# A new hand-written order for the first run of an attention and mixture-of-experts kernel, with other engines for some of its operations

## The chip, the core and the metric

The kernel runs on one core of a Trainium2 chip. The metric is the device time of one execution in microseconds (us). The kernel before takes 992.88 us, the median of three runs (991.37, 992.88 and 993.13). The profile is of one more execution, which took 993.18 us.

## The reference

The computation is causal attention over 4 batches, 8 heads, 576 positions and 64 dimensions per head, mixed per head with a linear memory branch, and then four experts over all 2304 rows of the result:

```python
a = softmax(causal(scale * q @ k.T));  local = a @ v        # per batch and head
phi = lambda x: where(x > 0, x, exp(x) - 1) + 1
mem = (phi(q) @ M_prev) / (phi(q) . z_prev + 1e-6)
g = 1 / (1 + exp(-beta))
x = (g * mem + (1 - g) * local)          # to (B*S, H*D) = (2304, 512)
p = probs / (probs.sum(-1) + 1e-9)
out = sum over 4 experts e of p[:, e] * (relu(x @ w1[e]) @ w2[e])   # 512 -> 1024 -> 512
```

Everything is float32. The expert products are computed as three products of a high part and a low part of each operand (`xh`, `xl`, `w`, `hh`, `hl`).

## The kernel before, in words

The order of all work is written by the kernel itself; no scheduler reorders it. The attention is cut into runs of one batch and two or three blocks of 128 positions. The expert work is cut into phases: a phase takes half an expert's hidden units, computes `h` (`mm1`, matmuls at L889, evicted by ScalarE as `hh` at L898 and by VectorE as `hl` at L899) and then `y` (`mm2`, L920). The weights come by DMA into `stg`, and `w_prep` (L212) splits each 128x512 piece into a high part (L227 on Pool, or L225 on ScalarE) and a low part (L228 on Pool). While TensorE works at the phases, the attention of later runs is put between their matmuls by a planner with costs and due times; its tasks are pairs of heads of a run (`t_trq`, `t_trk`, `t_phi1` to `t_phi4`, `j_qk` and so on).

The phases need a first run of attention to start on: batch 0, positions 0 to 255, all 8 heads. This is `first_run` (L1253). Its order is the list of words `ORDER`, and each word with its number is a call of a local function: `tr` transposes q and k of a pair of heads, `cq` and `ck` bring them from PSUM to SBUF, `sc` multiplies them (pair 0..3 and query block 0..1 make the numbers 0..7), `mk` masks and takes the row maximum on VectorE, `ex` is the exponential with its sum on ScalarE, `rc` the reciprocals on VectorE, `nm` the scaling of the exponentials by 1/sum on ScalarE (L1350; 16 of them, one for each of the 8 blocks and 2 heads), `pt` and `pe` transpose the probabilities and evict them, `r`, `e`, `p`, `z`, `rr`, `rn`, `m` are the memory branch (z and m on Pool, p, rr, rn on VectorE), `tq` and `eq` transpose its q and evict it, `ou` multiplies with the values and the memory, `xh` and `xl` split the result, `w` is one `w_prep` (both parts on Pool), `go` runs the planner's steps that are due before the first phase, and `d` is a pair of dummy matmuls of zeros, 128x512, on TensorE.

The first task of the next run (index 0) starts within the first run by `go`: `t_phi2` puts `qp` on VectorE (L314) and `zb`, `rl` on Pool (L319, L323, L326), and `t_phi3` puts the reduction `rn` on VectorE (L339). `t_trq` and `t_trk` of this task transpose its q and k (`tq`, `tk`), split them on ScalarE and VectorE (L366, L369, L372, L379, L385), and `t_cpk` copies halves of `khb` and `kha` by DMA on ScalarE's queue. Its first scores are `sp` (L486).

In PSUM, `h` and `y` share the tag `moe`, which has three banks: the fourth `h` of a phase takes the bank of the first, once `hh` and `hl` of the first have been read from it. The `after()` call in `mm1` issues a planner's step that follows the `h`. `c_probs2` (L868 to L873) normalises the experts' probabilities on VectorE (`psm`, `pn`). The start of the kernel has the zeros for the dummies, the identity and the masks; six dummy matmuls `ids` stand ahead of the list.

Of the kernel before, what the change touches and what calls it, by code (L numbers as in the profile page):

```python
# [10 lines left out]
AF = mybir.ActivationFunctionType  # L11
ALU = mybir.AluOpType
# [37 lines left out]
def tile_attention_moe(  # L50
# [344 lines left out]
    def flat(ap):  # L395
        return ap.rearrange("p j d -> p (j d)")

    def t_trq(t):
        pt = to_tile(f"tq{t.i}")
        qk, last = t.qk, t.nk == NCH  # L400
        w = len(t.cs) * P
        for i in range(len(t.cs)):

            tr(pt[:, i * P : (i + 1) * P], flat(t.nat["q"][:, i]), P)
        if last:
            tr(pt[:, w : w + P], flat(t.nat["k"][:, 4]), P)
# [341 lines left out]
    def ev(slot, prio, fn, cost=0.0, vec=0.0):  # L748
        wt = PR["wvec"] + PR["wpe"] * cost + vec
        events.setdefault(slot, []).append((prio, len(events.get(slot, [])), fn, wt))  # L750

    def dv(n):
        return 150.0 + n / 0.96

    seen = set()
    for t in tasks:
        s0 = t.s0
        ld = -9 + t.i if t.i < 2 else s0 - 7
        PQ = PR
        n = len(t.cs)  # L760
        if t.run not in seen:
            seen.add(t.run)
            ev(s0 - 9, 9 if t.i else 6, lambda r=t.run: batch_load(r))
            ev(s0 - (5 if t.i else 8), 9, lambda r=t.run: batch_load_m(r))
            ev(s0 + (2 if t.joint else 3), 9 if t.joint else 0.1, lambda r=t.run: batch_prep(r))
            if t.cs == CB and t.b == 0:
                for i in range(2):
                    ev(s0 - 12, 9, lambda i=i: zeros(i))
        if t.joint:
            ev(ld, 6.3, lambda t=t: t_load(t))  # L770
        else:
# [12 lines left out]
        ev(s0 + PQ["trq"][0], PQ["trq"][1], lambda t=t: t_trq(t), 109.0 * n, 2 * dv(n * P))
        ev(s0 + PQ["trk"][0], PQ["trk"][1], lambda t=t: t_trk(t), 109.0 * t.nk, 2 * dv(4 * P))
        if not t.joint:
            ev(s0 + PQ["trq"][0] + 1, 0.5, lambda t=t: t_cpq(t))
            ev(s0 + PQ["trk"][0], 2.4, lambda t=t: t_cpk(t))
        ev(s0, PQ["v"], lambda t=t: t_v(t))
        ev(  # L790
            s0 + PQ["trqp"][0 if t.joint else 2],
            PQ["trqp"][1],
            lambda t=t: t_trqp(t),
            109.0 * n,
            2 * dv(t.nq),
        )
# [446 lines left out]
    def first_run():  # L1243
# [9 lines left out]
        qT, kT, tf, pf, st, ptp, pw, tpf, of = ({} for _ in range(9))  # L1253
        qpw = [xr[:, a, 4 * P : 6 * P] for a in range(NPAIR)]

        def load(dst, src, c, h0, h1):
            nc.sync.dma_start(
                out=dst[:, c, h0:h1],
                in_=src[b, h0:h1, c * P : (c + 1) * P].rearrange("h p d -> p h d"),
            )  # L1260
# [87 lines left out]
        def f_nm(i, hd):  # L1348
# [2 lines left out]
                s_[:, hd], s_[:, hd], AF.Copy, scale=t_[:, 4 + hd : 5 + hd]  # L1351
            )

        def f_pt(i):
            s_ = st[i][0]
            c = i % 2
            ptp[i] = (
                moe_bank(f"ptf{i}")
                if c
                else ps.tile([P, 512], F32, tag="pt", name=f"ptf{i}", bufs=1)  # L1360
            )
            pt4 = ptp[i][:, 0 : 2 * (c + 1) * P].rearrange("p (h j q) -> p h j q", h=2, q=P)
            for hd in range(2):
                for j in range(c + 1):
                    tr(pt4[:, hd, j], s_[:, hd, j * P : (j + 1) * P], P)

        def f_pe(i):
            n = 2 * (i % 2 + 1) * P
            t_ = sp.tile([P, DM], F32, tag="acc", name=f"ptw{i}", bufs=4)
            if i % 2:  # L1370
                nc.vector.tensor_copy(t_[:, 0:n], ptp[i][:, 0:n])
            else:
                nc.scalar.activation(t_[:, 0:n], ptp[i][:, 0:n], AF.Copy)
# [70 lines left out]

        def f_w(j):
            w_prep(0, "1" if j < HF else "2", True)
            if j in (1, 3):
                while si[0] < len(steps) and steps[si[0]][0] <= (-9 if j == 1 else -8):
                    run_step()

        def f_go(j):
            while si[0] < len(steps) and steps[si[0]][0] <= -j:
                run_step()

        def f_d(j):
            z_ = moe_bank(f"id{j}")
# [1 line left out]
                nc.tensor.matmul(z_, lhsT=hh[0][:, 0:P], rhs=hh[0], start=True, stop=True)  # L1458

        ORDER = """  # L1460
        tr0 cq0 ck0 sc0 mk00 ex00 mk01 sc1 tr1 mk10 ex01 d11 mk11 rc0 ex10 cq1 ex11
        ck1 d4 nm00 sc3 rc1 nm01 r1 sc2 pt0 e1 nm10 tr3 mk20 mk30 mk21 mk31 tr2 nm11
        pt1 ck3 cq2 p1 ck2 pe1 sc4 mk40 r0 mk41 d0 d1 e0 z1 d6 ex31 ex21 p0 d13 d8
        ex20 d3 ex30 rr1 z0 rc2 ex40 d7 d10 cq3 d5 nm21 pe0 ex41 rc3 rn1 rr0 ldv w0
        rc4 sc5 nm20 pt2 rn0 sc7 m1 mk50 nm30 nm31 m0 sc6 mk51 pe2 pt3 nm40 nm41
        ex50 ex51 tq0 w1 mk70 pe3 mk71 w2 rc5 eq0 tq1 eq1 w3 ex70 pt4 mk60 ou0 w4 d9
        ex71 nm51 tq3 mk61 xh0 nm50 rc7 xl0 eq3 d2 ex61 nm71 pt5 ex60 rc6 nm70 pe4
        nm60 nm61 pe5 tq2 ou1 pt7 w5 eq2 pt6 pe7 xh1 ou2 xl1 pe6 w6 ou3 go5 xh2 xl2
        xh3 xl3 go4 w7 d12
        """  # L1470
        calls = {k[2:]: g for k, g in locals().items() if k.startswith("f_")}

        nc.scalar.dma_start(out=betab, in_=beta.partition_broadcast(P))
        nc.scalar.activation(psm[:, 0:1], ident[:, 0:1], AF.Exp)
        for h0, h1 in ((0, 2), (2, 4), (4, 8)):
            for c in range(2):
                load(qF, q, c, h0, h1)
                load(kF, k, c, h0, h1)
        nc.sync.dma_start(out=zb, in_=z_prev[b : b + 1].partition_broadcast(P)[:, 0])
        for _ in range(NSTG):  # L1480
            w_dma()
# [152 lines left out]
```

## Time and profile before

| | us |
|---|---|
| median of 3 runs | 992.88 (991.37 to 993.13) |
| the profiled execution | 993.18 |
| its span in the profile | 991.4 |
| TensorE (PE) busy | 982.5 |
| VectorE (DVE) busy | 648.2 |
| Pool busy | 591.3 |
| ScalarE (ACT) busy | 567.0 |
| first expert matmul `h` starts (from the start of the span) | 32.78 |
| first expert matmul `y` starts | 40.40 |

The profiled execution is 1.78 us longer than its span. Times in the rows are counted from the start of the span. A row of the timeline reads: start, duration (of all instructions in the row, from the first start to the last end), engine, line, operation, output and input tiles, form, count, and in brackets the idle time of that engine just before with what ended it. The ends of matmuls are modelled: the distance between two starts is the better measure of what one costs.

### The profile page before, as it was taken

Reading aid. Unit: us, or ns where it says so; the run is one execution under the profiler, and the core shown is the slowest. Engines: PE = TensorE matmul, PEld = TensorE weight load, DVE = VectorE, ACT = ScalarE, POOL = GpSimd, SP = SyncE. Lnnn points to the kernel's source line nnn. Section 1 sums busy time; section 2 is a strip of 40 time slices with the busy share of each in tenths; the row PEclk is TensorE's granted clock in tenths of the full one; section 3 lists DMA queues with packets and bytes.
Section 4 is the critical chain, followed back from the end, with each engine's and each line's share of the span. In section 5 each row is a group of like instructions: output and inputs, shape, how many; then the busy total and the mean of one; then the engine's idle time right before and its main releaser. Section 6 shows DMA issues by size and latency. Waiting matters only on the chain.

```text
span 991.4 us, 16041 instructions
## 1 busy us (share of the span) xinstructions
PE 982.5 (99%) x5118; PEld 825.3 (83%) x5118; DVE 648.2 (65%) x1668; ACT 567.0 (57%) x1350; POOL 591.3 (60%) x601
## 2 busy tenths in 40 slices
PE   8999999999999999999999999999999999999998
PEld 6899878878888888888888888888888888888887
DVE  6788888887877788877777787745244153442533
ACT  7787866766666677866666665544324243242430
POOL 5898856666754667955665465486363562645620
PEclk9999999999999999999999999999999999999999
DMA  6766554454443356554543332141111111111102
GB/s 154 180 191 176 136 147 128 130 142 120 129 115 98 93 140 185 165 134 108 124 124 102 91 100 77 44 137 55 53 54 43 54 54 54 54 42 54 54 1 85
DMA packets 185268, 102.16 MB, mean 103 GB/s; under 512 B 96224, under 2 KB 163552, under 8 KB 185184
## 3 DMA queue, kind: packets, MB, share of 16 engines
q1 hardware_dynamic: 184880, 101.00, 37.5%
q8 instruction: 41, 0.67, 0.3%
q14 instruction: 43, 0.35, 0.1%
q10 hardware_dynamic: 304, 0.14, 0.1%
HBM read 90.09 MB, written 4.72 MB: 96 GB/s over the span
## 4 chain that ended last, share of the span: by engine, by line
PE 92%; DVE 3%; issue 1%; ACT 1%; DMA 1%; POOL 1%; POOLq 0%; ACTq 0%; DVEq 0%
PE h L889 21%; PE y L920 20%; PE y L1197 18%; PE x L1119 9%; PE z L1119 4%; PE pt L353 4%; PE sp L624 4%; PE o L734 3%; PE y L1119 2%; PE o L572 1%; PE sp L486 1%; PE tk L353 1%; PE tq L353 1%; PE tp L353 1%; PE id L1458 1%
## 5 line engine op out<-in xcount | busy, mean ns | idle before, releaser
L228 POOL TENSOR_TENSOR w2l<-stg,w2h 128x512 fp32r<-128x512 f32 x128 | 167.6, 1314 | 153.3 <-ACT w2h L225 148.6
L889 PE MATMUL h<-xh,w 128*128 128x512 f32 (+1 forms) x768 | 245.8, 370 | 0.0
L228 POOL TENSOR_TENSOR w<-stg,w 128x512 fp32r<-128x512 f32 x96 | 126.8, 1325 | 147.8 <-ACT w L225 130.2
L889 PEld LDWEIGHTS h<-xh,w 128*128 128x128 f32 x768 | 138.7, 189 | 17.6 <-POOL w L228 0.3
L889 PE MATMUL h<-xl,w 128*128 128x512 f32 (+1 forms) x384 | 136.4, 355 | 0.0
L920 PE MATMUL y<-w2h,hh 128*128 128x512 f32 x320 | 135.7, 424 | 0.1
L920 PE MATMUL y<-w2h,hl 128*128 128x512 f32 x320 | 126.3, 395 | 0.0
L920 PE MATMUL y<-w2l,hh 128*128 128x512 f32 x320 | 125.9, 393 | 0.2
L1214 DVE SCALAR_TENSOR_TENSOR acc<-y,pn,acc 128x512 f32<-128x512 f32 (+1 forms) x57 | 41.6, 740 | 82.3 <-PE y L1197 82.3
L673 ACT ACTIVATE pth<-pt 128x384 fp32r<-128x384 f32 (+3 forms) x128 | 50.3, 420 | 62.7 <-PE pt L353 61.6
L889 PEld LDWEIGHTS h<-xl,w 128*128 128x128 f32 x384 | 72.9, 190 | 5.8
L920 PEld LDWEIGHTS y<-w2h,hl 128*128 128x128 f32 x320 | 60.0, 188 | 14.3 <-DVE hl L899 0.8
L898 ACT ACTIVATE hh<-h 128x512 fp32r<-128x512 f32 (+1 forms) x96 | 50.4, 525 | 36.4 <-PE h L889 34.5
L920 PEld LDWEIGHTS y<-w2l,hh 128*128 128x128 f32 x320 | 60.6, 189 | 9.5 <-POOL w2l L228 2.4
L920 PEld LDWEIGHTS y<-w2h,hh 128*128 128x128 f32 x320 | 60.4, 189 | 8.1 <-issue 0.5
L899 DVE SCALAR_TENSOR_TENSOR hl<-h,hh 128x512 fp32r<-128x512 f32 (+1 forms) x96 | 57.5, 599 | 13.3 <-ACT hh L898 11.9
L353 PE MATMUL pt<-ident,s 128*128 128x128 f32 (+1 forms) x376 | 60.8, 272 | 0.2
L353 PEld LDWEIGHTS pt<-ident,s 128*128 128x128 f32 (+1 forms) x376 | 46.9, 139 | 14.2 <-ACT s L669 0.5
L1143 DVE TENSOR_TENSOR cp_a<-y,cp_a 128x512 f32<-128x512 f32 x16 | 11.1, 692 | 71.4 <-PE y L1119 71.4
L225 ACT ACTIVATE w<-stg 128x512 fp32r<-128x512 f32 x92 | 57.0, 625 | 0.7
L675 DVE TENSOR_TENSOR ptl<-pt,pth 128x384 fp32r<-128x384 f32 (+1 forms) x96 | 51.5, 550 | 8.1 <-ACT pth L673 5.6
L648 ACT ACTIVATE s<-s,st 128x384 f32<-128x384 f32 (+2 forms) x80 | 54.7, 684 | 2.2 <-DVE st L632 1.9
(274 smaller groups left out, 2570.5 us busy)
## 6 DMA issues: line engine op xcount, KB each, us to landing
stg<-in_moe_w_dram SPq DMA_DIRECT2D x256, 256.0 KB, 2.9
natall<-in_k_dram SPq DMA_DIRECT2D x34, 128.0 KB, 2.6
natall<-in_v_dram SPq DMA_DIRECT2D x32, 128.0 KB, 3.1
natall<-in_q_dram SPq DMA_DIRECT2D x60, 64.0 KB, 2.8
out_dram<-acc SPq DMA_DIRECT2D x15, 256.0 KB, 2.0
kha<-kha SPq DMA_DIRECT2D x16, 128.0 KB, 2.3
khb<-khb SPq DMA_DIRECT2D x16, 128.0 KB, 2.3
natall<-in_k_dram SPq DMA_DIRECT2D x28, 64.0 KB, 2.6
```

What stands on the lines that cost most here:

```text
L225: nc.scalar.activation(hi, t, AF.Copy)
L228: nc.gpsimd.tensor_tensor(lo, t, f(hi), ALU.subtract)
L353: nc.tensor.transpose(dst, src, ident[0:n, 0:n])
L648: nc.scalar.activation(s.s[:, 0:w], s.s[:, 0:w], AF.Exp, bias=s.st[:, 0:1], scale=-1.0, accum_out=s.st[:, 2:3],)
L673: nc.scalar.activation(dh, src, AF.Copy)
L675: nc.vector.tensor_tensor(dl, src, f(dh), ALU.subtract)
L889: nc.tensor.matmul(pt[0][:, cols], lhsT=w_[:, c], rhs=x_[:, c, cols], start=(c == 0 and z == 0), stop=(c == NKD - 1 and z == 2),)
L898: nc.scalar.activation(h_, pt[0][:, cols], AF.Relu)
L899: nc.vector.scalar_tensor_tensor(l_, pt[0][:, cols], 0.0, f(h_), ALU.max, ALU.subtract)
L920: nc.tensor.matmul(pt[0], lhsT=h_[fc][:, tk], rhs=w_, start=(fc == 0 and z == 0), stop=(fc == HF - 1 and z == 2),)
L1119: nc.tensor.matmul(k_, lhsT=w_[:, c], rhs=x_[:, c], start=new and n == 0, stop=n == 5, skip_group_check=True,)
L1197: nc.tensor.matmul(y0, lhsT=a[:, tk], rhs=w_[:, x0:x1], start=(fc == 0 and z == 0), stop=(fc == HF - 1 and z == 2),)
```

## The change

The change replaces `ORDER` and adds functions for its new words. Of the 16 scalings, nine are done by Pool (`np`), two by VectorE (`nd`), five stay with ScalarE (`nm`). The scaled q of pairs 0 and 1 is evicted by VectorE (`cv`) instead of ScalarE, all four k by ScalarE (`ka`) instead of VectorE; the evictions of probabilities are five on ScalarE and three on VectorE instead of four and four, those of the memory branch's q two and two instead of four on ScalarE. The first task's `tk`, `kh`, `kl`, `tx`, `qh`, `ql` are words of the list now, and the planner's events for them are dropped. The first two loads of k are issued on ScalarE's queue, ahead of its table load, and the load of beta on Pool's queue. There are two pairs of dummies ahead of the list instead of three, and 14 within it as before. The word `w1` no longer issues planner steps; `go9` does. Cut to its core:

```diff
@@ planner @@
-        ev(s0 + PQ["trq"][0], PQ["trq"][1], lambda t=t: t_trq(t), 109.0 * n, 2 * dv(n * P))
-        ev(s0 + PQ["trk"][0], PQ["trk"][1], lambda t=t: t_trk(t), 109.0 * t.nk, 2 * dv(4 * P))
+        if t.i:
+            ev(s0 + PQ["trq"][0], PQ["trq"][1], lambda t=t: t_trq(t), 109.0 * n, 2 * dv(n * P))
+            ev(
...
@@ first_run @@
+        def f_cv(a):
+            nc.vector.tensor_scalar(qT[a], tf[a][0][:, 0:GW], SCALE, None, ALU.mult)
+        def f_ka(a):
+            by_act(kT[a], tf[a][1][:, 0:GW])
+        def f_np(i, hd):
+            s_, t_ = st[i]
+            nc.gpsimd.tensor_scalar(
+                s_[:, hd], s_[:, hd], t_[:, 4 + hd : 5 + hd], 1.0, ALU.mult, ALU.mult
+            )
+        def f_nd(i, hd):
+            s_, t_ = st[i]
+            nc.vector.tensor_scalar(
+                s_[:, hd],
+                s_[:, hd],
+                t_[:, 4 + hd : 5 + hd],
+                None,
+                ALU.mult,
+                ALU.max,
+                accum_out=dump,
+            )
         def f_w(j):
             w_prep(0, "1" if j < HF else "2", True)
-            if j in (1, 3):
-                while si[0] < len(steps) and steps[si[0]][0] <= (-9 if j == 1 else -8):
-                    run_step()
+            if j == 3:
+                f_go(8)
+        def f_tk(i):
+            tp_["k"] = to_tile("tk0")
+            for c in range(2):
+                tr(tp_["k"][:, c * P : (c + 1) * P], flat(tasks[i].nat["k"][:, c]), P)
+        def f_kh(i):
+            k_hi(tp_["k"], tasks[i].qk, 0, GW)
+            t_cpk(tasks[i])
+        def f_kl(i):
+            k_lo(tp_["k"], tasks[i].qk, 0, GW, True)
...
         ORDER = """
-        nm60 nm61 pe5 tq2 ou1 pt7 w5 eq2 pt6 pe7 xh1 ou2 xl1 pe6 w6 ou3 go5 xh2 xl2
-        xh3 xl3 go4 w7 d12
...
+        rc2 np30 ex40 tq0 nm31 eq1 nd20 w0 pt3 mk50 eq0 tq3 np21 mk51 ex41 ex50 rc4
+        ex51 ev3 pa3 rc5 ou0 pt2 mk60 xh0 pv2 np41 np40 nm50 tq2 mk61 sc7 xl0 pt4
+        mk70 ex60 mk71 ev2 ex61 np51 w1 pt5 pv4 ou1 w2 w3 pa5 ex71 rc6 ex70 w4 w5 ou2
+        rc7 xh1 nm61 xl1 w6 nm71 nm60 nd70 pt7 pt6 xh2 pa7 xl2 tk0 kh0 pv6 ou3 kl0
+        xh3 tx0 qh0 xl3 d12 w7 d3 d11 ql0 go5 go4
         """
-        nc.scalar.dma_start(out=betab, in_=beta.partition_broadcast(P))
+        for c in range(2):
+            load(kF, k, c, 0, 2, nc.scalar)
         nc.scalar.activation(psm[:, 0:1], ident[:, 0:1], AF.Exp)
         for h0, h1 in ((0, 2), (2, 4), (4, 8)):
             for c in range(2):
                 load(qF, q, c, h0, h1)
-                load(kF, k, c, h0, h1)
+                if h0:
+                    load(kF, k, c, h0, h1)
...
-        for j in range(3):
+        for j in range(2):
             f_d(f"s{j}")
...
     make_identity(nc, ident)
+    nc.gpsimd.dma_start(out=betab, in_=beta.partition_broadcast(P))
```

What this does to Pool's row of instructions is seen at two places. The first is Pool's memory branch and first weights. L1390 is `z` and L1405 is `m` (L1430 and L1445 after the change); `w` and `stg` are a `w_prep`; `sf` is a block of exponentials, scaled by L1369 after the change. Before:

```order
L1390 TENSOR_TENSOR xr<-xr,zbf 128x4x128 x2
L227 TENSOR_SCALAR w_109<-stg_159 128x512
L228 TENSOR_TENSOR w_109<-stg_159,w_109 128x512
L1405 TENSOR_TENSOR xr<-xr,rnf_143 128x4x128
L1405 TENSOR_TENSOR xr<-xr,rnf_142 128x4x128
```

After:

```order
L1369 TENSOR_SCALAR sf_203<-sf_203,stf_204 128x128 x2
L1369 TENSOR_SCALAR sf_225<-sf_225,stf_226 128x256 x2
L1430 TENSOR_TENSOR xr<-xr,zbf 128x4x128 x2
L1445 TENSOR_TENSOR xr<-xr,rnf_144 128x4x128
L1445 TENSOR_TENSOR xr<-xr,rnf_143 128x4x128
L1369 TENSOR_SCALAR sf_258<-sf_258,stf_259 128x256
L227 TENSOR_SCALAR w_109<-stg_159 128x512
L228 TENSOR_TENSOR w_109<-stg_159,w_109 128x512
L1369 TENSOR_SCALAR sf_274<-sf_274,stf_275 128x128
L1369 TENSOR_SCALAR sf_343<-sf_343,stf_344 128x128 x2
L1369 TENSOR_SCALAR sf_388<-sf_388,stf_389 128x256
```

Four scalings stand ahead of `z` now, and five behind `m`, around the first `w_prep`.

The second place is Pool's last two weights of the first run and the first task's memory branch (`zb`, `rl`). Before:

```order
L227 TENSOR_SCALAR w2h_114<-stg_421 128x512
L228 TENSOR_TENSOR w2l_115<-stg_421,w2h_114 128x512
L319 TENSOR_TENSOR zb_0_405<-zb_0_405,gate 128x512
L323 TENSOR_TENSOR rl_554<-qp_553,zb_0_405 128x4x64
L326 TENSOR_SCALAR rl_554<-gate 128x4
L227 TENSOR_SCALAR w2h_116<-stg_433 128x512
L228 TENSOR_TENSOR w2l_117<-stg_433,w2h_116 128x512
L345 TENSOR_TENSOR qp_553<-qp_553,rn_596 128x256
```

After:

```order
L227 TENSOR_SCALAR w2h_114<-stg_470 128x512
L228 TENSOR_TENSOR w2l_115<-stg_470,w2h_114 128x512
L227 TENSOR_SCALAR w2h_116<-stg_474 128x512
L228 TENSOR_TENSOR w2l_117<-stg_474,w2h_116 128x512
L319 TENSOR_TENSOR zb_0_331<-zb_0_331,gate 128x512
L323 TENSOR_TENSOR rl_578<-qp_577,zb_0_331 128x4x64
L326 TENSOR_SCALAR rl_578<-gate 128x4
L345 TENSOR_TENSOR qp_577<-qp_577,rn_583 128x256
```

The eighth `w_prep` stood behind `rl`, and stands ahead of it now.

The third place is VectorE around the first `hl`, which frees the PSUM bank for the fourth `h`. L899 is L906 after the change, L870 to L873 are L877 to L880. `rn` reads the `rl` of Pool. Before:

```order
L339 TENSOR_REDUCE rn_596<-rl_554 128x4
L340 RECIPROCAL rn_596<-rn_596 128x4
L899 SCALAR_TENSOR_TENSOR hl_105<-h_0_586,hh_101 128x256
L870 TENSOR_REDUCE psm<-pn 128x8
L871 TENSOR_SCALAR psm<-psm 128x8
L872 RECIPROCAL psm<-psm 128x8
L873 TENSOR_TENSOR pn<-pn,psm 128x32
L314 SCALAR_TENSOR_TENSOR qp_616<-natall,ex_613 128x256
```

After:

```order
L339 TENSOR_REDUCE rn_583<-rl_578 128x4
L340 RECIPROCAL rn_583<-rn_583 128x4
L877 TENSOR_REDUCE psm<-pn 128x8
L878 TENSOR_SCALAR psm<-psm 128x8
L879 RECIPROCAL psm<-psm 128x8
L880 TENSOR_TENSOR pn<-pn,psm 128x32
L314 SCALAR_TENSOR_TENSOR qp_604<-natall,ex_598 128x256
L906 SCALAR_TENSOR_TENSOR hl_105<-h_0_586,hh_101 128x256
```

`hl` stood directly behind `rn`, and now has the four instructions of the experts' probabilities and the next `qp` ahead of it.

## Rows read from the trace of the kernel before

**Rows 1.** The page, parts 1 and 4: busy time of the engines; chain that ended last.

```profile
PE 982.5 (99%) x5118; PEld 825.3 (83%) x5118; DVE 648.2 (65%) x1668; ACT 567.0 (57%) x1350; POOL 591.3 (60%) x601
...
PE 92%; DVE 3%; issue 1%; ACT 1%; DMA 1%; POOL 1%; POOLq 0%; ACTq 0%; DVEq 0%
```

**Rows 2.** Busy time by stretch: length, then each engine, granted clock, DMA share, GB/s.

```profile
0.00:5.24 5.24, 3.78 (x10) 2.72 (x10) 1.78 (x6) 2.18 (x5) 3.66 (x15) 1.00 0.38 83
...
32.78:40.40 7.62, 6.78 (x57) 6.62 (x57) 6.46 (x21) 4.19 (x14) 6.62 (x11) 1.00 0.85 206
40.40:100.00 59.60, 59.27 (x410) 53.67 (x409) 49.46 (x173) 48.26 (x130) 51.59 (x54) 1.00 0.65 177
100.00:991.40 891.40, 886.55 (x4484) 743.64 (x4482) 571.63 (x1392) 490.77 (x1132) 511.73 (x506) 1.00 0.35 95
```

**Rows 3.** Timeline of TensorE from 29.5 to 48 us.

```profile
32.78 0.36 PE L889 MATMUL h<-xh,w 128*128 128x256 f32 x1
...
37.95 0.30 PE L486 MATMUL sp<-khb,qb 128*128 128x128 f32 x1 [0.84 <-DMA khb<-khb]
...
38.19 0.33 PE L889 MATMUL h<-xh,w 128*128 128x256 f32 x1
...
40.40 0.40 PE L920 MATMUL y<-w2h,hh 128*128 128x512 f32 x1
```

**Rows 4.** Timeline of Pool from 0 to 40 us.

```profile
13.69 1.27 POOL L1390 TENSOR_TENSOR xr<-xr,zbf 128x512 f32<-128x512 f32 x1 [9.28 <-DVE xr L1386]
15.77 1.29 POOL L1390 TENSOR_TENSOR xr<-xr,zbf 128x512 f32<-128x512 f32 x1 [0.81 <-DVE xr L1386]
...
34.02 0.73 POOL L323 TENSOR_TENSOR rl<-qp,zb 128x256 f32<-128x256 f32 x1
34.81 0.20 POOL L326 TENSOR_SCALAR rl<-gate 128x4 f32<-128x4 f32 x1
35.10 0.62 POOL L227 TENSOR_SCALAR w2h<-stg 128x512 fp32r<-128x512 f32 x1
...
37.06 0.62 POOL L345 TENSOR_TENSOR qp<-qp,rn 128x256 f32<-128x256 f32 x1
...
39.23 0.40 POOL L448 TENSOR_SCALAR v<-natall 128x256 fp32r<-128x256 f32 x1
```

**Rows 5.** Timeline of VectorE from 27 to 42 us.

```profile
29.56 1.53 DVE L314 SCALAR_TENSOR_TENSOR qp<-natall,ex 128x256 f32<-128x256 f32 x1 [0.36 <-ACT ex L308]
...
35.39 0.42 DVE L339 TENSOR_REDUCE rn<-rl 128x4 f32<-128x260 f32 x1
...
36.05 0.42 DVE L899 SCALAR_TENSOR_TENSOR hl<-h,hh 128x256 fp32r<-128x256 f32 x1
36.40 0.17 DVE L870 TENSOR_REDUCE psm<-pn 128x8 f32<-128x32 f32 x1
...
37.64 0.41 DVE L314 SCALAR_TENSOR_TENSOR qp<-natall,ex 128x256 f32<-128x256 f32 x1
```

**Rows 6.** Timeline of TensorE from 0 to 16 us.

```profile
1.45 2.93 PE L1458 MATMUL ids<-hh 128*128 128x512 f32 x6 [1.45 <-DVE hh L1500]
4.17 0.63 PE L353 MATMUL tf<-ident,natall 128*128 128x128 f32 x2
...
5.84 1.65 PE L1294 MATMUL pf<-tw,tw 64*128 64x128 f32 x8 [0.61 <-DVE tw L1283]
...
14.50 1.86 PE L1458 MATMUL id<-hh 128*128 128x512 f32 x7
```

**Rows 7.** Timeline of SyncE's queue to 14 us, the load of z_prev.

```profile
6.96 0.50 SPq L1479 DMA_DIRECT2D zbf<-in_z_prev_dram  x1
```

**Rows 8.** DMA issues to 20 us: KB each, median us from issue to landing.

```profile
zbf<-in_z_prev_dram SPq DMA_DIRECT2D x1, 256.0 KB, 4.8
```

**Rows 9.** Timeline of ScalarE to 9 us, the first reader of beta.

```profile
3.77 0.21 ACT L1487 ACTIVATE ebp<-betab 128x8 f32<-128x8 f32 x1 [1.06 <-DMA betab<-in_beta_dram]
```

**Rows 10.** All executions of L1350 (`nm`): duration ns least/median/most, first and last start.

```profile
L1350 ACT ACTIVATE sf<-sf,stf x16: 388/447/505, 9.2 to 27.5; 128x128 f32<-128x128 f32 x8, 128x256 f32<-128x256 f32 x8
```

More of the change, by code (lines that the diff above doesn't have):

```diff
@@ L783, in tile_attention_moe @@
         ev(s0 - 3, 20, lambda t=t: t_phi4(t))
-        ev(s0 + PQ["trq"][0], PQ["trq"][1], lambda t=t: t_trq(t), 109.0 * n, 2 * dv(n * P))
-        ev(s0 + PQ["trk"][0], PQ["trk"][1], lambda t=t: t_trk(t), 109.0 * t.nk, 2 * dv(4 * P))
+        if t.i:
+            ev(s0 + PQ["trq"][0], PQ["trq"][1], lambda t=t: t_trq(t), 109.0 * n, 2 * dv(n * P))
+            ev(
+                s0 + PQ["trk"][0],
+                PQ["trk"][1],
+                lambda t=t: t_trk(t),
+                109.0 * t.nk,
+                2 * dv(4 * P),
+            )
         if not t.joint:
@@ L1254, in first_run, with load @@
         qpw = [xr[:, a, 4 * P : 6 * P] for a in range(NPAIR)]
-        def load(dst, src, c, h0, h1):
-            nc.sync.dma_start(
+        def load(dst, src, c, h0, h1, eng=nc.sync):
+            eng.dma_start(
                 out=dst[:, c, h0:h1],
@@ L1352, in f_nm @@
             )
+        def f_np(i, hd):
[13 more added lines that the diff above has]
+                accum_out=dump,
+            )
         def f_pt(i):
@@ L1367, in f_pe, with f_pv, f_pa, by_act @@
         def f_pe(i):
+            (f_pv if i % 2 else f_pa)(i)
+        def f_pv(i):
+            out_pt(i, nc.vector.tensor_copy)
+        def f_pa(i):
+            out_pt(i, by_act)
+        def by_act(d, src):
+            nc.scalar.activation(d, src, AF.Copy)
+        def out_pt(i, copy):
             n = 2 * (i % 2 + 1) * P
             t_ = sp.tile([P, DM], F32, tag="acc", name=f"ptw{i}", bufs=4)
[L1370 to L1373, printed above, removed]
+            copy(t_[:, 0:n], ptp[i][:, 0:n])
             pw[i] = t_[:, 0:n].rearrange("p (h j q) -> p h j q", h=2, q=P)
@@ L1421, in f_eq, with f_ev @@
             nc.scalar.activation(qpw[a], tpf[a][:, 0:GW], AF.Copy)
+        def f_ev(a):
+            nc.vector.tensor_copy(qpw[a], tpf[a][:, 0:GW])
         def f_ou(a):
@@ L1453, in f_go, with f_tx, f_qh, f_ql @@
                 run_step()
+        tp_ = {}
+        def f_tk(i):
[7 more added lines that the diff above has]
+            k_lo(tp_["k"], tasks[i].qk, 0, GW, True)
+        def f_tx(i):
+            tp_["q"] = to_tile("tq0")
+            for c in range(2):
+                tr(tp_["q"][:, c * P : (c + 1) * P], flat(tasks[i].nat["q"][:, c]), P)
+        def f_qh(i):
+            q_hi(tp_["q"], tasks[i].qk["qa"], tasks[i].qk["qb"], GW, SCALE)
+        def f_ql(i):
+            q_lo(tp_["q"], tasks[i].qk["qa"], tasks[i].qk["qb"], GW, SCALE)
         def f_d(j):
@@ L1460, in first_run @@
         ORDER = """
[L1461 to L1467, printed above, removed]
-        nm60 nm61 pe5 tq2 ou1 pt7 w5 eq2 pt6 pe7 xh1 ou2 xl1 pe6 w6 ou3 go5 xh2 xl2
-        xh3 xl3 go4 w7 d12
+        tr0 ka0 d7 d4 cv0 sc0 mk00 tr1 mk01 ex00 ka1 ex01 sc1 d1 mk10 mk11 ex10 d6 d2
+        ex11 cv1 sc3 d13 rc0 r1 np01 np00 e1 rc1 r0 np10 np11 mk30 mk31 pt0 p1 e0 d10
+        sc2 mk20 d5 mk21 tr2 p0 cq2 z1 tr3 ka2 ex30 d0 z0 d9 rr1 rn1 rr0 ka3 d8 sc4
+        pt1 cq3 ldv go9 rn0 pa0 mk40 ex31 sc5 mk41 sc6 ex21 ex20 m1 rc3 m0 pa1 tq1
+        rc2 np30 ex40 tq0 nm31 eq1 nd20 w0 pt3 mk50 eq0 tq3 np21 mk51 ex41 ex50 rc4
[3 more added lines that the diff above has]
+        xh3 tx0 qh0 xl3 d12 w7 d3 d11 ql0 go5 go4
         """
         calls = {k[2:]: g for k, g in locals().items() if k.startswith("f_")}
-        nc.scalar.dma_start(out=betab, in_=beta.partition_broadcast(P))
+        for c in range(2):
+            load(kF, k, c, 0, 2, nc.scalar)
         nc.scalar.activation(psm[:, 0:1], ident[:, 0:1], AF.Exp)
```

## The prediction

> **What bounds the kernel now.** I read the page first. TensorE is busy for 982.5 of 991.4 us, and the chain that ended last is 92% TensorE [rows 1]: the reader is to see that nothing but TensorE's own work and its few gaps counts. The second view is busy time by stretch [rows 2]. From 40.40 to 100 us TensorE idles for 59.60 - 59.27 = 0.33 us, from 100 us to the end for 891.40 - 886.55 = 4.85 us, half a per cent. From 32.78 to 40.40 it idles for 0.84 us, and the timeline shows that this is a single wait: the scores `sp` wait for the copy of `khb` [rows 3]. So behind 40.40 us, where the first `y` starts, there is almost no slack in which a delay could be lost or a lead be wasted. The change is confined to the work ahead, and the total of matmuls behind stays the same. The question of this prediction is therefore one number: when does the first `y` start? Each us there is a us of the kernel.
>
> The third view is who is late ahead of that `y`. TensorE starts the first `h` at 32.78, and four groups of twelve matmuls follow, with the scores between. From 38.19 to 40.40 stand 18 matmuls of `h` [rows 3], 0.123 us each, so a group is 1.47 us and the fourth starts at 40.40 - 1.47 = 38.93. It reuses the bank of the first `h`, which is free when `hl` has read it: 36.05 + 0.42 = 36.47 [rows 5]. That is a slack of 2.46 us. `hl` stands behind `rn` in VectorE's order, and `rn` reads Pool's `rl`, which ends at 34.81 + 0.20 = 35.01 [rows 4]. Pool is the engine to watch: after the memory branch's `z` starts at 13.69, it has one gap, 0.81 us, and then works without a pause up to there [rows 4]. From 13.69 to 35.01 are 21.32 us, 20.51 of them work.
>
> **The change part by part.** *Start.* Three pairs of dummies become two ahead of the list; two pairs (`d7`, `d4`) now stand between the first transposes and the first scores, where a wait of 0.61 us stood. Six dummies take 2.93 us at the start, 0.49 each, and seven take 1.86, 0.27 each, at 14.50 [rows 6]: near 1.2 and 2.4 GHz. The granted clock of the first 5.24 us reads 1.00 all the same [rows 2], so I go by the durations; between the two, the engine had only short gaps. Two removed dummies give 0.98, four inserted ones cost 1.96 less the wait of 0.61 that they fill, so the first scores come 0.4 later at the slow level (earlier by about half of it if the higher level comes before they run). The first transposes can begin earlier than 4.17 [rows 6], since two of the four loads that they wait for move to a second queue; the gain is between nothing and the 0.98 that the dummies leave. I take these as cancelling.
>
> *Loads.* On SyncE thirteen issues end with that of `zbf`, at 6.96 + 0.50 = 7.46 [rows 7], 0.57 each. Two fewer stand ahead of it, so it is issued 1.1 earlier, and its landing moves from 6.96 + 4.8 = 11.76 [rows 7, 8] to 10.6. The load of beta moves to Pool's queue. Its first reader ran at 3.77 after a wait [rows 9], and now the first eviction of q on VectorE stands behind the same chain; that eviction follows the first transposes, which started at 4.17 in before. It has about 1 us of cover. If the load lands 2 us later, 1 us of delay is left for the whole first run. I cost it at nothing and keep that 1 us for the range.
>
> *Scalings.* ScalarE loses eleven, at 0.447 us the median [rows 10] 4.9 us, of a queue that no step of this sum waits for behind the start. The trace of before has no such scaling on Pool. Nearest are Pool's operations with one tensor input: 0.40 us for 256 columns (L448), 0.62 for 512 (L227) [rows 4], so on a straight line 0.29 for 128. The upper bound is the operation with two inputs, 0.73 for 256 (L323) [rows 4], half of that for 128. The lower is 0.20, for 4 columns (L326). I take the line, since the scaling has one tensor input. Four of the nine stand ahead of `z`, when Pool idles. The five behind (two of 256, three of 128 columns) add 2 x 0.40 + 3 x 0.29 = 1.67 us to Pool's full stretch; by the upper bound 2.6, by the lower 1.0.
>
> *Pool's order.* The eighth `w_prep` now stands ahead of `zb` and `rl`. It takes 37.06 - 35.10 = 1.96 us [rows 4], and `rl` comes that much later. Pool's work from `z` to the end of `rl` becomes 20.51 + 1.67 + 1.96 = 24.14.
>
> *When `z` starts.* It waits for `p` on VectorE, for `zbf`, and now for the four scalings. It cannot start before 10.6 (the landing), and with the new words `r1`, `e1`, `p1` ahead of most of the masking it should not start later than the 13.69 of before. The middle is 12.15; I take 12.4, a little nearer to the row. The gap of 0.81 between the two `z` is covered by `m` or by a scaling only in part, and the five scalings each wait for exponentials and a reciprocal: 0.3 us of new waits, between 0 and 1. So `rl` ends at 12.4 + 24.14 + 0.3 = 36.8.
>
> *VectorE's order.* Behind `rl` stand `rn` (36.05 - 35.39 = 0.66), then, new ahead of `hl`, the probabilities and the next `qp` (from 36.40 to 37.64 + 0.41 = 38.05, 1.65), then `hl`, 0.42 [rows 5]. The bank is free at 36.8 + 2.73 = 39.5, and the fourth `h` cannot start earlier, wherever the first `h` began. The first `y` starts 1.47 later, at 41.0, against 40.40. The two transposes of `tq` for the second task stand behind `y` in before and within the fourth `h` now, and cancel.
>
> *First task's q and k.* With the transposes of k inside the first run the copy of `khb` is issued earlier and the wait of 0.84 [rows 3] goes; but what is gained there stands ahead of the fourth `h`, and is spent waiting for the bank. The same goes for any earlier first `h`. That is the heart of the forecast: TensorE may well begin its first `h` one or two us sooner, and stop in front of the fourth.
>
> Sum: +0.6 on the profiled execution, 993.18 + 0.6 = 993.8. That execution lies 0.30 above the median of 992.88, so for the median I say 993.5.
>
> *A rule beside this.* One `qp` (L314) took 1.53 us at 29.56, while the same line took 0.41 at 37.64 [rows 5]. The Trainium skill (SBUF — State Buffer, "SBUF: two separate sides") says that VectorE and GpSimd share a pair of ports as an exclusive lock, which an instruction of VectorE with two SBUF inputs or one of GpSimd holds for its whole length while the other blocks. The slow row agrees with it, the other does not show it, although Pool worked at 37.06 to 37.68 [rows 4]. With the lock in the way the new `qp` ahead of `hl` would be 1.53 - 0.41 = 1.12 longer and the time 994.6; without it the sum stands.
>
> **The rivals.** *Pool is later still: slower.* `z` starts no earlier than in before (+1.29), the scalings wait 1 us in all (+0.7), or cost what the two-input operation does (+0.9), or the long `qp` falls into the chain (+1.12). All four together are +4.0, 997.5; two of them, which I hold for likely if any, are about +2.1, 995.6. It decides from the point where `rl` ends after 38.2 (1.4 later than in my sum). For it: Pool has no gap to give, and each of the nine scalings waits for two other engines. Against: ScalarE and VectorE have fewer evictions and scalings ahead of the exponentials.
>
> *The bank does not bind: faster.* If Pool reaches `rl` by about 34, the fourth `h` starts when TensorE gets there. With the first `h` at 31.0 (the 0.61 and about a us of other fill gone), three groups, the transposes and scores (4.4 + 0.7) put the fourth at 36.1 and the first `y` at 37.7, 2.7 earlier: 990.2 for the median. It needs `z` at its earliest, 10.6, where the sum gives `rl` at 34.7 and the bank at 37.5 without waits, or scalings that fall into gaps of Pool. For it: Pool's row gives `z` a wait of 9.28 for VectorE, so there is room ahead. Against: 24.14 us of work that cannot start before the landing. At that earliest point the first `y` starts at about 39.0, and the median is 991.5.
>
> *The change cancels itself.* The first run ends within 0.3 us of where it did, because Pool's lead by an earlier `z` just pays for `w_prep` and scalings: 992.9. The planner's later events shift as well, since two of them are dropped, with 5.2 us of idle time in all behind 40.40 [rows 2] as the most that they could touch.
>
> **How the numbers follow.** The forecast of 993.5 with its own range 991.5 to 995.0 has a chance of 0.42, the change that cancels itself 0.12, the bank that does not bind 0.20, the later Pool 0.26. About 0.2% (2 us, 990.9 to 994.9) is what a measurement of this kernel tells from no change. Faster takes the rival's 0.20 and 0.02 from the forecast's lower edge: 0.22. Slower takes the rival's 0.26 less 0.03 for its mildest cases, and 0.05 from the forecast's upper edge: 0.28. The rest is 0.50. The range reaches to the two rivals' main prices, 990.2 and 995.6, with some room above for three of the four delays: 990.0 to 996.5.
>
> **What the profile after would show.** Right: first `h` earlier than 32.78; no wait of `sp` for `khb`; a gap of TensorE of some us in front of the fourth `h`, put down to VectorE's `hl`; `rl` ending near 36.8 and behind the eighth `w_prep`; the first `y` near 41.0; hardly any idle time behind. Wrong: no gap there, or a `y` ahead of 39; `rl` ahead of 35; or a gap of more than a us elsewhere behind 41 us.

## The result, and the profile after

The kernel after takes 999.42 us (median of 6 runs, 999.14 to 999.92), the kernel before 992.84 beside it (6 runs). The ratio is 1.0069, with a 95% interval of 1.0056 to 1.0082: slower by 6.6 us, where 0.6 were forecast. The profiled execution took 999.14, its span is 997.3.

The page after, parts 1, 4 and 5, the lines that answer to [rows 1]:

```profile
PE 982.8 (99%) x5116; PEld 825.6 (83%) x5116; DVE 650.3 (65%) x1671; ACT 564.2 (57%) x1340; POOL 596.5 (60%) x611
...
PE 89%; POOL 4%; issue 2%; DVE 2%; ACT 1%; DMA 0%; SPq 0%; POOLq 0%; DVEq 0%
...
L896 PE MATMUL h<-xh,w 128*128 128x512 f32 (+1 forms) x768 | 245.9, 371 | 4.8 <-DVE hl L906 4.6
```

TensorE's work is the same within 0.3 us, the span is 5.9 longer, and Pool's share of the chain went from 1 to 4%. The group of `h` has 4.8 us of idle time before it now, 4.6 of them one wait for `hl`; the same line of the page before had none:

```profile
L889 PE MATMUL h<-xh,w 128*128 128x512 f32 (+1 forms) x768 | 245.8, 370 | 0.0
```

TensorE's timeline after shows where the wait is, to be read against [rows 3]:

```profile
31.33 0.28 PE L896 MATMUL h<-xh,w 128*128 128x256 f32 x1
...
34.23 0.28 PE L486 MATMUL sp<-khb,qb 128*128 128x128 f32 x1
...
41.01 0.36 PE L896 MATMUL h<-xh,w 128*128 128x256 f32 x1 [4.56 <-DVE hl L906]
...
43.72 0.63 PE L927 MATMUL y<-w2h,hh 128*128 128x512 f32 x1
```

The first `h` starts 1.45 us earlier than before, `sp` no longer waits for `khb`, and the fourth `h` waits 4.56 us. The first `y` starts at 43.72 instead of 40.40. Behind the wait the `h` and `y` are slow, and the busy time by stretch after says why (columns as in [rows 2]; the granted clock is the third number from the right):

```profile
36.40:41.00 4.60, 0.05 (x1) 0.02 (x1) 2.23 (x9) 0.00 (x0) 3.06 (x6) 1.00 0.27 62
...
41.60:43.72 2.12, 2.12 (x12) 2.12 (x11) 1.99 (x12) 1.66 (x7) 1.14 (x2) 0.50 0.00 0
43.72:44.97 1.25, 1.25 (x4) 0.99 (x4) 1.18 (x6) 1.04 (x3) 0.03 (x1) 0.52 0.49 109
44.97:47.00 2.03, 2.03 (x13) 1.73 (x12) 1.60 (x7) 0.44 (x2) 1.85 (x2) 1.00 0.39 104
```

TensorE starts again at 41.01, for half a us still at 1.00. From 41.60 to 44.97 the granted clock is 0.50 and 0.52, that is 1.2 GHz, and from there 1.00, that is 2.4 GHz.

Pool's timeline after, answering to [rows 4]:

```profile
12.47 1.28 POOL L1430 TENSOR_TENSOR xr<-xr,zbf 128x512 f32<-128x512 f32 x1 [0.62 <-DVE xr L1426]
14.38 1.28 POOL L1430 TENSOR_TENSOR xr<-xr,zbf 128x512 f32<-128x512 f32 x1 [0.63 <-DVE xr L1426]
16.07 1.04 POOL L1445 TENSOR_TENSOR xr<-xr,rnf 128x512 f32<-128x512 f32 x1 [0.40 <-DVE rnf L1440]
17.52 1.04 POOL L1445 TENSOR_TENSOR xr<-xr,rnf 128x512 f32<-128x512 f32 x1 [0.41 <-DVE rnf L1440]
18.53 0.48 POOL L1369 TENSOR_SCALAR sf<-sf,stf 128x256 f32<-128x256 f32 x1
...
20.96 1.62 POOL L1369 TENSOR_SCALAR sf<-sf,stf 128x128 f32<-128x128 f32 x4
...
34.47 0.62 POOL L227 TENSOR_SCALAR w2h<-stg 128x512 fp32r<-128x512 f32 x1
...
38.37 0.20 POOL L326 TENSOR_SCALAR rl<-gate 128x4 f32<-128x4 f32 x1
```

`z` starts at 12.47. Behind it come three gaps (0.63, 0.40, 0.41), five scalings, eight `w_prep`, and `rl`, which ends at 38.57. The row x4 merges two shapes, three scalings of 128 columns and one of 256; all nine, by shape:

```profile
L1369 POOL TENSOR_SCALAR sf<-sf,stf x9: 361/372/479, 10.2 to 22.1; 128x128 f32<-128x128 f32 x5, 128x256 f32<-128x256 f32 x4
```

VectorE's timeline after, answering to [rows 5], shows VectorE waiting for the end of `rl`:

```profile
38.60 0.42 DVE L339 TENSOR_REDUCE rn<-rl 128x4 f32<-128x260 f32 x1 [5.95 <-POOL rl L326]
...
39.15 0.15 DVE L877 TENSOR_REDUCE psm<-pn 128x8 f32<-128x32 f32 x1
...
40.00 0.41 DVE L314 SCALAR_TENSOR_TENSOR qp<-natall,ex 128x256 f32<-128x256 f32 x1
40.44 0.42 DVE L906 SCALAR_TENSOR_TENSOR hl<-h,hh 128x256 fp32r<-128x256 f32 x1
```

One more loss lies later. TensorE's waits over the whole span after (total, times, longest) have a line that the kernel before has not, and the longest of the four waits is at 108.63:

```profile
PE y L927 <- POOL w2l L228: 2.0, 4, 0.9
```

```profile
108.63 0.50 PE L927 MATMUL y<-w2l,hh 128*128 128x512 f32 x1 [0.87 <-POOL w2l L228]
```

The other three lie between 377 and 411 us. Reading TensorE's starts in both traces along the program, the kernel after is behind by 3.3 us at the first `y`, 4.1 at the `h` of the second phase, and 5.4 at the last matmul (993.31 against 987.90). The last 0.5 of the 5.9 us comes behind that matmul, up to the end of the span (4.0 us instead of 3.5); no run shows why.

### The profile page after: what moved, and what is told of

The parts are those of the page before. It is cut to its first block, busy times and chain, and to the rows that moved or that the text cites. A ratio compares the mean times of both kernels' runs of the same rounds, so it can differ in the third digit from the quotient of the medians.

```text
span 997.3 us, 16048 instructions
## 1 busy us (share of the span) xinstructions
PE 982.8 (99%) x5116; PEld 825.6 (83%) x5116; DVE 650.3 (65%) x1671; ACT 564.2 (57%) x1340; POOL 596.5 (60%) x611
## 4 chain that ended last, share of the span: by engine, by line
PE 89%; POOL 4%; issue 2%; DVE 2%; ACT 1%; DMA 0%; SPq 0%; POOLq 0%; DVEq 0%
PE h L896 20%; PE y L927 20%; PE y L1204 17%; PE x L1126 9%; PE z L1126 4%; PE pt L353 4%; PE sp L624 4%; PE o L734 4%; PE y L1126 2%; POOL w2l L228 2%; POOL w L228 1%; PE o L572 1%; PE tk L353 1%; PE sp L486 1%; PE tq L353 1%
## 5 line engine op out<-in xcount | busy, mean ns | idle before, releaser
L228 POOL TENSOR_TENSOR w2l<-stg,w2h 128x512 fp32r<-128x512 f32 x128 | 167.8, 1315 | 157.3 <-ACT w2h L225 151.7
L228 POOL TENSOR_TENSOR w<-stg,w 128x512 fp32r<-128x512 f32 x96 | 126.6, 1323 | 147.9 <-ACT w L225 123.8
L906 DVE SCALAR_TENSOR_TENSOR hl<-h,hh 128x512 fp32r<-128x512 f32 (+1 forms) x96 | 57.5, 599 | 12.8 <-ACT hh L905 11.5
L943 DVE SCALAR_TENSOR_TENSOR acc<-y,pn,acc 128x512 f32<-128x512 f32 x70 | 52.1, 744 | 7.1 <-PE y L927 6.5
```

What stands on the lines that cost most here:

```text
L228: nc.gpsimd.tensor_tensor(lo, t, f(hi), ALU.subtract)
L906: nc.vector.scalar_tensor_tensor(l_, pt[0][:, cols], 0.0, f(h_), ALU.max, ALU.subtract)
L943: nc.vector.scalar_tensor_tensor(acc[g, tt], pt[0], pe, acc[g, tt], ALU.mult, ALU.add)
```

## The experiments

The kernel before took 991.92 us (median) beside the first eight of the twelve runs, 991.94 beside the next two and 992.35 beside the last two, against 992.84 beside the kernel after. So gains are read from the ratios to it; the kernel after stands at 1.0069.

**`rl` ahead of the eighth `w_prep` again.**

```diff
-        xh3 tx0 qh0 xl3 d12 w7 d3 d11 ql0 go5 go4
+        xh3 tx0 qh0 xl3 d12 go5 w7 d3 d11 ql0 go4
```

> The kernel after the change, with go5 (qp, zb and rl of the first task) ahead of the eighth w_prep again; all else as changed. Theory (the fourth h waits for the bank that hl frees, hl stands behind rn, rn behind Pool's rl): rl ends 1.96 us earlier, at 36.6 instead of 38.57, the fourth h starts at 39.0 instead of 41.01, the wait is 2.6 instead of 4.56 us, and the time falls from 999.4 to 997.5; if the shorter wait also spares the slow matmuls behind it (12 of h and 3 of y at about half rate, 1.6 us), to 995.9. Rival (the loss comes from the scalings on Pool and the later order, and the wait in front of the fourth h is only where it shows): 999.4 again, with the wait shrunk and other waits grown.

Measured: 997.12, ratio 1.0052 (1.0038 to 1.0065), 1.7 us less than the kernel after. Its TensorE:

```profile
39.25 0.36 PE L896 MATMUL h<-xh,w 128*128 128x256 f32 x1 [3.04 <-POOL qp L345]
41.92 0.63 PE L927 MATMUL y<-w2h,hh 128*128 128x512 f32 x1
```

`rl` ended at 36.20, and the first `y` came 1.8 us earlier; 0.3 of both belong to this execution's earlier start (`z` at 12.18). The clock was still lowered (group of `h` 2.67 us). The place of `w_prep` is worth about what it takes on Pool.

**Empty planner events for the two dropped ones.**

```diff
+        else:
+            ev(s0 + PQ["trq"][0], PQ["trq"][1], lambda: None, 109.0 * n, 2 * dv(n * P))
+            ev(s0 + PQ["trk"][0], PQ["trk"][1], lambda: None, 109.0 * t.nk, 2 * dv(4 * P))
```

> The kernel after the change, with the two dropped planner events of the first task put back as empty events of the same cost, so that they issue nothing and only the planner's count is as before. Theory: hl stands directly behind rn again, ahead of the probabilities and the next qp, so it ends at 39.7 instead of 40.86 and the fourth h starts at 39.8 instead of 41.01: 1.2 us less; and if the 2.0 us in which y waits for w2l later come from the shifted order, they go too: 996.5 in all. Rival (the planner's shift is harmless, later waits come from Pool being late): 998.2 with the later waits unchanged.

Measured: 996.51, ratio 1.0045 (1.0033 to 1.0058), 2.4 less, as forecast. `hl` follows `rn` directly, at 38.78; the fourth `h` starts at 39.35 (0.5 of the 1.66 is an earlier start, `z` at 11.96), and the waits of `y` for `w2l` are not in the trace. TensorE in the stretch from 100 to 200 us, in the kernel after, then in this one:

```profile
100.00:200.00 100.00, 98.39 (x542) 82.61 (x542) 84.72 (x278) 70.62 (x186) 67.66 (x79) 1.00 0.49 129
```

```profile
100.00:200.00 100.00, 99.35 (x541) 82.60 (x541) 83.38 (x271) 71.60 (x188) 68.50 (x79) 1.00 0.52 135
```

So two things hung on the planner's count of work: `hl`'s place on VectorE, and waits of TensorE some 65 to 370 us behind the first `y`, of which the stretch above shows one us. The new `ORDER` by itself shows neither.

**Dummies in the wait.**

```diff
+            if c == 0 and i == 0 and fc == 3:
+                z_ = to_tile("idf")
+                for _ in range(20):
+                    nc.tensor.matmul(z_, lhsT=hh[0][:, 0:P], rhs=hh[0], start=True, stop=True)
```

> The kernel after the change, with 20 dummy matmuls of 128x512 (4.3 us at the fast rate) on TensorE between the third and the fourth h, in the time in which it waited 4.56 us. Theory (the idle time lowered the clock: granted clock 0.50 from 41.6 to 43.7): the fourth h still starts at about 41.0, but it and the first three y run at full rate: 1.6 us less, 997.8. Rival (the slow rows have another cause, such as Pool and VectorE at work beside them): the same rows stay slow, 999.4, or more if the dummies overrun the wait.

Measured: 997.55, ratio 1.0058 (1.0046 to 1.0071), 1.1 less by the ratios, where 1.6 were forecast. By stretch:

```profile
36.40:41.00 4.60, 4.56 (x21) 3.48 (x21) 2.46 (x10) 0.00 (x0) 3.07 (x5) 1.00 0.30 64
41.00:42.48 1.48, 1.48 (x15) 1.48 (x15) 1.45 (x7) 0.68 (x3) 1.25 (x4) 1.00 0.00 0
```

The fourth `h` starts at 40.76, nearly where it did, and the first `y` 1.72 us later, where the kernel after took 2.71. VectorE and ScalarE worked beside it as in the kernel after. So the slow rows come from the lowered clock, and the lowered clock from the idle time. The wait itself stays.

**The kernel before, with its eighth `w_prep` ahead of `zb` and `rl`.**

```diff
-        nm60 nm61 pe5 tq2 ou1 pt7 w5 eq2 pt6 pe7 xh1 ou2 xl1 pe6 w6 ou3 go5 xh2 xl2
-        xh3 xl3 go4 w7 d12
+        nm60 nm61 pe5 tq2 ou1 pt7 w5 eq2 pt6 pe7 xh1 ou2 xl1 pe6 w6 ou3 w7 go5 xh2 xl2
+        xh3 xl3 go4 d12
```

> The kernel before the change, with its eighth w_prep moved ahead of go5 (zb and rl), and nothing else. Theory: rl ends 1.96 us later, at 37.0; hl, directly behind rn there, ends at 38.05, still ahead of the 38.93 at which the fourth h starts: no wait, 992.8, the same as before. Rival (the place of the eighth w_prep alone is what costs): a wait in front of the fourth h or of the first y, 994 or more.

Measured: 992.07, ratio 1.0002 (0.9993 to 1.0011): no change, no wait in front of the fourth `h`. `rl` ended at 35.49 and not at 37.0, since `z` started at 12.16 in this execution, 1.53 us earlier than in [rows 4]; the first `h` moved by as much. The slack of the kernel before covers the move.

**Both repairs.** The two edits of the first two experiments together.

> The kernel after the change with both repairs: go5 ahead of the eighth w_prep, and empty planner events of the same cost for the two dropped ones, so that hl stands directly behind rn. Theory (a chain of rl, rn, hl and the bank): rl ends near 36.1 as with the first repair, hl near 37.3, the fourth h starts at 37.4 instead of 39.35, a wait of about 1.1 us; the first y at 39.0 to 39.5, the clock falls little or not, and the time is 992.5 to 993.5, about as before the change. Rival (the two repairs remove the same wait, so they do not add): 996, no better than the better of them.

Measured: 993.66, ratio 1.0015 (1.0006 to 1.0023), 5.4 less than the kernel after, just above the forecast range. The two gains alone were 1.7 and 2.4, so together they give more than their sum. What is left, on TensorE:

```profile
37.60 0.36 PE L899 MATMUL h<-xh,w 128*128 128x256 f32 x1 [1.26 <-DVE psm L880]
...
40.72 0.47 PE L930 MATMUL y<-w2h,hh 128*128 128x512 f32 x1 [1.45 <-DVE hl L909]
```

Waits of 1.26 and 1.45 us did not lower the clock (1.00 behind both); that this cost is gone too is the likely reason for more than the sum. The second wait is for the next `hl`, which has the probabilities and `qp` ahead of it.

**Both repairs, and `rn` behind the first `hl`.**

```diff
-            s0 + PQ["phi3"][0] if t.i else s0 - 3,
+            s0 + PQ["phi3"][0] if t.i else s0 - 0.6,
...
-        ev(s0 - 3, 20, lambda t=t: t_phi4(t))
+        ev(s0 - 3 if t.i else s0 - 0.5, 20, lambda t=t: t_phi4(t))
```

> As the kernel with both repairs, and with rn and the scaling of qp of the first task issued by the planner three slots later (rn stands behind the first hl, which then waits for nothing of Pool). Theory: no wait in front of the fourth h, which starts at about 36.0; the first y at 37.5 to 38.0; 991.0 to 991.6, faster than before the change (991.9) by 0.3 to 0.9. Rival (the next hl, behind rn, frees its bank too late for the first y, or Pool's late w_prep makes y wait): the wait moves in front of the first y, 992.5 to 993.5 as with both repairs alone.

Measured: 992.25, ratio 0.9999 (0.9991 to 1.0008). No wait in front of the fourth `h`; the first `y` starts at 38.40 after a wait of 0.64. The earlier `y` than in [rows 3] is not 2 us of gain against the kernel before: in the run with only the eighth `w_prep` moved, that kernel's order reached the first `y` at 39.22, since its first run was faster there. The forecast, faster by 0.3 to 0.9, missed; the time is that of the kernel before.

**Five scalings on ScalarE again, all else as after.**

```diff
-        rc2 np30 ex40 tq0 nm31 eq1 nd20 w0 pt3 mk50 eq0 tq3 np21 mk51 ex41 ex50 rc4
+        rc2 nm30 ex40 tq0 nm31 eq1 nd20 w0 pt3 mk50 eq0 tq3 nm21 mk51 ex41 ex50 rc4
...
```

(and `nm41`, `nm40`, `nm51` for `np41`, `np40`, `np51`)

> The kernel after the change with the five later scalings (30, 21, 41, 40, 51) on ScalarE again and four on Pool; the order of the words is unchanged. Theory (Pool's chain sets the fourth h): Pool has 2.1 us less, rl ends at 36.4 instead of 38.57, the fourth h starts at 38.9 instead of 41.01, and the time is 997.3, or 996.0 if the clock recovers sooner; a later first h (ScalarE has 2.2 us more) is hidden in the wait. Rival (ScalarE's load sets the fill): the first h at 33 or later and 999 or more.

Measured: 995.25, ratio 1.0032 (1.0019 to 1.0044), 3.7 less, below both forecasts. The first `h` is 1.6 us later, and it does not matter, since the wait absorbed it:

```profile
32.90 0.28 PE L896 MATMUL h<-xh,w 128*128 128x256 f32 x1
...
38.97 0.36 PE L896 MATMUL h<-xh,w 128*128 128x256 f32 x1 [0.94 <-DVE hl L906]
40.69 0.39 PE L927 MATMUL y<-w2h,hh 128*128 128x512 f32 x1
```

The gain is larger than the 2.1 us of Pool, because 0.94 us of idle time did not lower the clock. The four waits of `y` for `w2l` are still there, 1.9 us in all, which speaks against Pool's lateness in the first run as their source. The scalings on Pool bought an earlier first `h`, and cost time at the fourth, where it counts.

**The late `rn`, with those five scalings on ScalarE.**

> As the kernel with both repairs and the late rn, and the five later scalings on ScalarE again. If Pool is still what is late behind the repairs, this is faster than without by up to 1 us, 990.5; if ScalarE then delays the first h, slower by as much as the first h moves, 992 to 993; if neither is late, the same.

Measured: 992.00, ratio 1.0000 (0.9992 to 1.0009): the same as without. First `h` at 32.40, first `y` at 38.78, no wait between.

**`rn` behind the second `hl` too.** The slots `s0 - 0.6` and `s0 - 0.5` become `s0`, with priorities 0.5 and 0.6.

> As the kernel with both repairs, and with rn and the scaling of qp of the first task later still, behind the second hl: neither of the first two hl waits for Pool. Theory: no wait of TensorE in front of the fourth h nor of the first y (0.64 us in the run with the earlier rn); the first y at about 37.6, and with the 952.7 us that follow a first y in the undisturbed runs 990.3 to 990.9, 1.0 to 1.6 faster than before the change. Rival (something else is late then: the transposes of qp, which wait for Pool, or the w2l of the eighth w_prep): the first y at 37.6, but waits of 1 us or more behind it, 991.5 to 992.3.

Measured: 992.56, ratio 1.0004 (0.9995 to 1.0013): the forecast missed, its rival held. The first `y` starts at 37.51, but the transposes of `qp` wait 0.8 us for Pool behind it, those of k 0.4 for VectorE, and a `y` 0.3 for `w2l`. Its time is 0.3 above the rival's range too.

**The same with one scaling (51) on ScalarE.**

> As the run before it, with one more scaling (51) on ScalarE instead of Pool. If Pool is still late behind the first y (w2l), 0.3 us faster, 990.2 to 990.8; if ScalarE's 0.5 us more moves the first h, 0.5 slower, 991.0 to 991.6.

Measured: 993.13, ratio 1.0007 (0.9997 to 1.0016), not clear of the run beside it; the first `h` is 1.1 us later, at 31.96. Both forecasts missed, with times 1.5 us and more too low.

**Two pairs of dummies less**, and in a second kernel three, from the kernel with the late `rn` and five scalings on ScalarE.

```diff
-        xh3 tx0 qh0 xl3 d12 go5 w7 d3 d11 ql0 go4
+        xh3 tx0 qh0 xl3 d12 go5 w7 ql0 go4
```

> The kernel with both repairs, the late rn and five scalings back on ScalarE, less the two pairs of dummies d3 and d11 right ahead of the first h. That kernel's TensorE has no wait from there to the first y, so theory says that the dummies are on the path now: four of 0.23 us, first h at 31.5 instead of 32.40, first y at 37.9 instead of 38.78, 991.1 against 992.0, and 0.8 below the kernel before (991.9). Rival (the h then wait for the split of the result or the bank): the wait takes their place, 992.0.

> As the run beside it, less d12 too: nothing stands between the transposes of q and the first h. Theory: the h wait for the last split of the result or for the bank of the first h now, so nothing more is gained, 991.1; if not, 990.7. Rival (the idle time lowers the clock): 992 or more.

Measured: 991.19, ratio 0.9990 (0.9981 to 0.9999), and 991.48, ratio 0.9992 (0.9984 to 1.0001). With two pairs less TensorE has no wait from 31.13 to the first `y` at 38.16, and the time is the forecast one. It is the one kernel whose interval lies below 1, and only just: about a us faster than the kernel before. As it is the best of twelve, that is not firmly shown. The third pair gains nothing more.

## Why the prediction was wrong

The mechanism was the forecast one, to the place: an earlier first `h`, no wait for `khb`, then a stop in front of the fourth `h` for a bank that `hl` frees behind `rn`, `rl` and the eighth `w_prep`. Undoing any of its links gives time back. It was the size that failed, in three steps.

*`rl` at 36.8.* It ended at 38.57, 1.8 us later. The start of `z` was right (12.47 for 12.4), with luck, since 12.4 was a choice between 10.6 and 13.69. But the "0.3 us of new waits" on Pool were 0.63 + 0.40 + 0.41 = 1.44. The first is the gap between the two `z`, which nothing covered; in the other two `m` waits for `rn` of its own block, which waits for `z`, and the `w_prep` that filled this in the kernel before now stands behind. And the five scalings took 0.48 + 1.62 = 2.10 us instead of 1.67: 0.47 to 0.48 for 256 columns and not 0.40, 0.36 to 0.37 for 128 and not 0.29. So the line through the two operations of [rows 4] was too low at both shapes, by about 0.1 us for each scaling. This is the rival "Pool is later still", past its point of 38.2; I had given it 0.26, and even its price with all four delays, 997.5, falls short of 999.42. VectorE's chain behind was 2.26 us instead of 2.73, so the bank was free at 40.86.

The traces also point to what widened the three gaps. In the memory branch of the kernel after, three VectorE instructions on the way to the ends of the gaps ran long beside Pool:

```profile
12.99 1.31 DVE L1426 SCALAR_TENSOR_TENSOR xr<-natall,xr 128x512 f32<-128x512 f32 x1
...
14.93 0.75 DVE L1439 SCALAR_TENSOR_TENSOR rnf<-rnf,gate 128x8 f32<-128x8 f32 x1
...
16.51 0.62 DVE L1439 SCALAR_TENSOR_TENSOR rnf<-rnf,gate 128x8 f32<-128x8 f32 x1
```

The same two lines in the kernel before took as little as this (another L1399 took 0.58 there, beside Pool's L227):

```profile
15.00 0.69 DVE L1386 SCALAR_TENSOR_TENSOR xr<-natall,xr 128x512 f32<-128x512 f32 x1
...
18.80 0.25 DVE L1399 SCALAR_TENSOR_TENSOR rnf<-rnf,gate 128x8 f32<-128x8 f32 x1
```

The first ran on for 0.55 us behind the end of Pool's `z` (12.47 + 1.28 = 13.75). The other two ended at 15.68 and 17.13, with Pool's second `z` (14.38 + 1.28 = 15.66) and first `m` (16.07 + 1.04 = 17.11). They are 0.62, 0.50 and 0.37 us longer than the short ones, close to the three gaps; that the gaps would go with them is an estimate from these rows, and no run tests it. The prediction had put a price on such a long VectorE row, but at one place alone, the new `qp` ahead of `hl`, and there it cost nothing: `qp` took 0.41 at 40.00. Its row against (0.41 at 37.64 in [rows 5]) could not tell, since it overlaps Pool's by only 0.04 us.

*"The first `y` starts 1.47 later."* It came 2.71 later, the two transposes of `tq` (0.13) among them. Nothing in the sum said that a TensorE that stops for so long loses its clock: 12 matmuls of `h` and three `y` at 1.2 GHz cost about 1.1 and 0.55 us more. Filling the wait showed it. With this the first `y` is at 0.6 + 1.5 + 1.1 + 0.13 = 3.3 later, as measured.

*"Hardly any idle time behind", and the planner as a rival with no more than its 5.2 us.* The dropped events shifted which step goes behind which matmul; 2.0 us of waits for `w2l` came of it, and the kernel after loses another 1.3 us from the second phase to the last matmul. The kernel with the empty events lost 0.1 there. Idle time that a kernel has is also no bound on what a new order can add, and 3.2 of the 5.2 us lie behind the last matmul (987.90 + 0.28, of 991.40). I had seen the shift in VectorE's order, but took it for a part of the list and not for a change that goes on for 400 us.

Of the costs held at nothing, beta's was nothing: its first reader ran at 4.32, before the first transposes were done with. The start was not: the first scores came at 6.24, 0.4 us later, the figure worked out ahead of the cancelling.

The kernel before has a spread of its own. In its profiled execution the first `h` started at 32.78, in the run with only the eighth `w_prep` moved at 31.38, with the same instructions ahead. Four dummies took 2.05 us at 8.19 in the one and 1.33 at 7.34 in the other, near 1.2 and 2.4 GHz: TensorE came to the higher level later in the first. I took the slower one as the base; against the other, the kernel after starts its first `h` no earlier at all.

## What to carry to other kernels

A gain ahead of a wait is no gain: look for the next point where the engine at the limit takes a buffer, and follow who frees it through every queue, in the new order. A stop of TensorE costs more than its length when the clock falls with it: here stops of 3.0 to 4.6 us did that, and stops of 0.9 to 1.5 did not. If a long stop can't be removed, dummies in it keep the clock. Where a planner counts work, taking an item out of its list can move all that follows; leave its cost in. An instruction of VectorE can take longer beside one of Pool (1.31 us for 0.69 here), so the rows of both engines are to be read side by side when an order is priced.

## What the runs showed of the hardware

- TensorE's clock: after waits of 4.56, 3.43 and 3.04 us the granted clock was 0.50 in about three us of the work behind them (0.50 and 0.52 from 41.60 to 44.97 after the first); after 0.94, 1.26 and 1.45 us it stayed at 1.00. In the run with dummies in the wait it stayed at 1.00 too.
- Pool's scaling takes 0.36 to 0.37 us for 128x128 and 0.47 to 0.48 for 128x256: twice the columns cost 0.1 us more.
- VectorE beside Pool: besides the three rows of the memory branch above, the normalisation `pn` (L880), 128x32, took 0.90 us in the run with `rl` first, against 0.29 in the kernel after, and ended with the low part of the `w_prep` (L228) beside it. VectorE's row, then Pool's:

```profile
37.42 0.90 DVE L880 TENSOR_TENSOR pn<-pn,psm 128x32 f32<-128x32 f32 x1
```

```profile
36.98 1.29 POOL L228 TENSOR_TENSOR w2l<-stg,w2h 128x512 fp32r<-128x512 f32 x1
```

37.42 + 0.90 = 38.32 and 36.98 + 1.29 = 38.27. The Trainium skill (SBUF — State Buffer, "SBUF: two separate sides") gives the two engines one pair of ports under an exclusive lock; these two rows agree with it. By these rows the longer `pn` took 0.6 us of what the first repair could have given.
